# Two gated linear-attention blocks on one core: a rewrite with pk^T x in place of V, queries modulo 5, and a fixed instruction order of its own

## The chip, the cores and the metric

The kernel runs on 1 core of one Trainium2 chip. The time is device microseconds (us) of that core, the median of several executions. The core has five engines that run side by side: PE (TensorE, matmuls), DVE (VectorE), ACT (ScalarE), POOL (GpSimd) and SP (SyncE, which here only starts DMA transfers). A DMA can be started from SP or ACT, which feed hardware queues, or from POOL, which feeds a software queue. The span is the time from the first to the last instruction in the profile of one execution.

## The reference

Two blocks A and B take the same input x (2048 rows, 640 columns, bf16), each with weights of its own. There are 32 heads of 20 columns, and the attention is linear, so no softmax over rows.

```python
g = sigmoid((x * gate_w).sum(-1))                 # one gate per row
for X in (A, B):
    q, k, v = split(x @ wqkv_X)                   # 640 -> 3 x 640, 32 heads of 20
    phi = lambda t: where(t > 0, t + 1, exp(t)) + 1e-6
    pq, pk = phi(q), phi(k)
    kv  = einsum("sd,se->de", pk, v)              # per head, 20 x 20
    z   = pk.sum(rows)                            # per head, 20
    o   = (pq @ kv) / (pq @ z + 1e-6)
    out_X = o @ wo_X
out = g * out_A + (1 - g) * out_B
```

## The kernel before

It projects Q, K and V, keeps V in bf16, and forms K^T V per group of heads. K^T V is masked to its head blocks and multiplied by Wo into one matrix WP per block, so that the output is one product of scaled Q and WP. The scale (gate over denominator) has one value per head and row. A matmul with a 0/1 matrix ("expansion") spreads it over the 20 columns of each head, and DVE multiplies Q by it.

```python
# x transposed by DMA: 4 blocks of 512 rows, 5 instructions of 128 columns each, on SP
for c in range(NCC):
    prs.append((XT[:, c, 512*b : 512*b+512], xin[512*b : 512*b+512, 128*c : 128*c+128]))
# gate_w (1.2 KB) is queued on SP behind the first five of them; PE begins with it
# K and V together: 1280 columns per row tile, in groups of 512, 512 and 256
[(XT[:, c, xcols], WKV[:, c, 0:512]) for c in range(NCC)]      # ... and 512:1024, 1024:1280
# z: ones^T pk on PE;  K^T V: V^T pk on PE, 5 windows x 16 row tiles
[(V16[:, t, 128*c : 128*c+128], PK[:, t, lo:hi]) for t in range(NSC)]
# expansion on PE, scaling on DVE from PSUM
[(CB16[:, EB_OFF+128*k : EB_OFF+128*k+128], RB[X][:, b, :])]
```

Each engine is given its instructions in one fixed order, and the semaphore waits come from a helper that records who reads and writes what. All matmuls therefore carry the helper's line, L296.

## Time and profile before

| before | value |
|---|---|
| time | 254.73 us median of 3 (253.84 to 254.8) |
| span in the profile | 251.6 us |
| PE busy | 225.6 us, 90% of the span |
| DVE busy, ACT busy | 137.5 us, 96.6 us |
| matmuls | 1571 |

These are lines of the page of the kernel before: busy time, the span in 40 slices (each digit is tenths of a slice), and the engines' shares of the chain of waits that ended last.

```profile
span 251.6 us, 3909 instructions
PE 225.6 (90%) x1571; PEld 120.2 (48%) x1571; DVE 137.5 (55%) x323; ACT 96.6 (38%) x207; POOL 7.3 (3%) x11
PE   0499999999999999899999788987976399999995
PEclk9999999999999999999999999999999689999999
PE 82%; DVE 11%; SPq 2%; issue 2%; ACT 1%; DMA 1%; ACTq 0%; DVEq 0%
```

PE is the engine to relieve. Three stretches have holes: the first 10 us, a shallow one from 131 to 185 us (PE busy 47.8 of 54 us), and the digits 9763 near 190 us. The view of busy time by stretches puts numbers on them. Its columns are the stretch, its length, busy us of PE, weight loads, DVE, ACT and POOL (with counts), the granted clock, the DMA share and GB/s.

```profile
0.00:10.00 10.00, 0.53 (x4) 0.32 (x4) 0.46 (x4) 1.28 (x1) 7.32 (x11) 1.00 0.76 200
131.00:185.00 54.00, 47.80 (x374) 27.24 (x371) 34.35 (x82) 20.82 (x50) 0.00 (x0) 1.00 0.00 1
185.00:200.00 15.00, 9.23 (x111) 4.17 (x111) 12.82 (x35) 4.34 (x9) 0.00 (x0) 0.88 0.00 0
200.00:249.00 49.00, 48.17 (x335) 26.39 (x335) 13.98 (x32) 9.55 (x16) 0.00 (x0) 0.97 0.15 51
```

The timeline of the output stage shows what a matmul costs when nothing holds it up (start, us, engine, line, what, count).

```profile
204.90 1.24 PE L296 MATMUL ps<-WPA,PQA 128*128 128x512 bf16 x5
205.97 1.24 PE L296 MATMUL ps<-WPB,PQB 128*128 128x512 bf16 x5
207.05 0.44 PE L296 MATMUL ps<-WPA,PQA 128*128 128x128 bf16 x5
207.33 0.44 PE L296 MATMUL ps<-WPB,PQB 128*128 128x128 bf16 x5
207.61 0.59 PE L296 MATMUL ps<-RBB,CB 128*128 128x512 bf16 x2
```

Read the starts, not the durations, since matmuls overlap. Five of 512 columns start 1.07 us apart, 215 ns each. Five of 128 columns start 0.28 us apart, 56 ns each. A pair of 512 and 128 columns is thus 0.271 us.

### The profile page before, as it was taken

Reading aid. Unit: us, or ns where it says so; the run is one execution under the profiler, and the core shown is the slowest. Engines: PE = TensorE matmul, PEld = TensorE weight load, DVE = VectorE, ACT = ScalarE, POOL = GpSimd, SP = SyncE. Lnnn points to the kernel's source line nnn. Section 1 sums busy time; section 2 is a strip of 40 time slices with the busy share of each in tenths; the row PEclk is TensorE's granted clock in tenths of the full one; section 3 lists DMA queues with packets and bytes.
Section 4 is the critical chain, followed back from the end, with each engine's and each line's share of the span. In section 5 each row is a group of like instructions: output and inputs, shape, how many; then the busy total and the mean of one; then the engine's idle time right before and its main releaser. Section 6 shows DMA issues by size and latency. Waiting matters only on the chain.

```text
span 251.6 us, 3909 instructions
## 1 busy us (share of the span) xinstructions
PE 225.6 (90%) x1571; PEld 120.2 (48%) x1571; DVE 137.5 (55%) x323; ACT 96.6 (38%) x207; POOL 7.3 (3%) x11
## 2 busy tenths in 40 slices
PE   0499999999999999899999788987976399999995
PEld 0244445555555449445555444543853055555553
DVE  0159996345345873596478686774359814242300
ACT  2045555665665530256655445452033011211111
POOL 8300000000000000000000000000000000000000
PEclk9999999999999999999999999999999689999999
DMA  7644694000000700000000000000000001111121
GB/s 217 143 103 101 153 384 168 1 0 0 3 0 0 261 3 0 3 0 0 3 3 0 0 3 0 0 3 0 0 3 0 3 26 52 54 54 52 55 78 52
DMA packets 17219, 12.43 MB, mean 49 GB/s; under 512 B 11249, under 2 KB 15858, under 8 KB 17202
## 3 DMA queue, kind: packets, MB, share of 16 engines
q1 hardware_dynamic: 16466, 10.98, 14.6%
q10 hardware_dynamic: 656, 0.82, 1.1%
q0 software_dynamic: 80, 0.39, 0.4%
q8 instruction: 12, 0.20, 0.3%
q14 instruction: 5, 0.04, 0.1%
HBM read 6.94 MB, written 2.62 MB: 38 GB/s over the span
## 4 chain that ended last, share of the span: by engine, by line
PE 82%; DVE 11%; SPq 2%; issue 2%; ACT 1%; DMA 1%; ACTq 0%; DVEq 0%
PE ps L296 82%; SPq L284 2%; DVE RBB L671 2%; DVE PK L519 2%; DVE RC L640 1%; DVE PQA L726 1%; DVE PQB L726 1%; DVE EK L510 1%; DMA GWROW<-in_gate_w_dram 1%; ACT EK L489 1%; DVE WPB L708 1%; DVE PK L533 0%; DVE RBA L658 0%; DVE ZBD L611 0%; ACT DT L633 0%
## 5 line engine op out<-in xcount | busy, mean ns | idle before, releaser
L296 PE MATMUL ps<-WKV,XT 128*128 128x512 bf16 (+1 forms) x480 | 88.8, 344 | 0.0
L296 PEld LDWEIGHTS ps<-WKV,XT 128*128 128x128 bf16 x480 | 46.7, 98 | 41.2
L417 ACT ACTIVATE EQ<-ps 128x512 bf16<-128x512 f32 x40 | 23.9, 597 | 43.2 <-PE ps L296 39.3
L510 DVE TENSOR_SCALAR EK<-EK 128x640 bf16<-128x640 bf16 x32 | 10.5, 327 | 38.3 <-ACT EK L489 38.3
L482 ACT ACTIVATE EK<-ps 128x512 bf16<-128x512 f32 x32 | 19.1, 597 | 26.0 <-PE ps L296 18.0
L296 PE MATMUL ps<-WPA,PQA 128*128 128x512 bf16 (+1 forms) x160 | 28.0, 307 | 0.8 <-DVE PQB L726 0.8
L296 PE MATMUL ps<-WPB,PQB 128*128 128x512 bf16 (+1 forms) x160 | 27.2, 301 | 0.0
L760 ACT ACTIVATE OSTG<-ps 128x512 bf16<-128x512 f32 x16 | 9.6, 597 | 45.0 <-PE ps L296 45.0
L296 PE MATMUL ps<-XT,WQA 128*128 128x512 bf16 x100 | 24.9, 411 | 0.0
L767 DVE CAST OSTG<-ps 128x128 bf16<-128x128 f32 x16 | 4.7, 292 | 35.0 <-PE ps L296 35.0
L519 DVE SCALAR_TENSOR_TENSOR PK<-ps,EK 128x512 bf16<-128x512 f32 x32 | 22.1, 692 | 1.1
L296 PE MATMUL ps<-XT,WQB 128*128 128x512 bf16 x100 | 21.9, 379 | 0.3 <-DVE ZBD L611 0.3
L296 PEld LDWEIGHTS ps<-WPA,PQA 128*128 128x128 bf16 x160 | 13.5, 99 | 13.0 <-DVE PQB L726 1.3
L296 PEld LDWEIGHTS ps<-WPB,PQB 128*128 128x128 bf16 x160 | 13.1, 99 | 9.9 <-issue 0.8
L296 PEld LDWEIGHTS ps<-XT,WQA 128*128 128x128 bf16 x100 | 10.1, 104 | 13.2 <-issue 3.5
L424 DVE TENSOR_SCALAR EQ<-EQ 128x512 bf16<-128x512 bf16 x40 | 11.5, 288 | 8.7 <-ACT EQ L417 7.0
L496 ACT ACTIVATE V<-ps 128x384 bf16<-128x384 f32 x32 | 15.7, 490 | 1.0
L296 PEld LDWEIGHTS ps<-XT,WQB 128*128 128x128 bf16 x100 | 9.7, 98 | 11.7 <-DVE ZBD L611 0.4
L489 ACT ACTIVATE EK<-ps 128x128 bf16<-128x128 f32 x32 | 8.9, 277 | 15.4 <-PE ps L296 14.9
L433 DVE SCALAR_TENSOR_TENSOR PQB<-ps,EQ 128x512 bf16<-128x512 f32 x20 | 13.8, 692 | 0.7
L433 DVE SCALAR_TENSOR_TENSOR PQA<-ps,EQ 128x512 bf16<-128x512 f32 x20 | 13.8, 692 | 0.7
L726 DVE TENSOR_TENSOR PQA<-PQA,ps 128x512 bf16<-128x512 bf16 x20 | 12.9, 680 | 1.0 <-PE ps L296 1.0
(54 smaller groups left out, 166.5 us busy)
## 6 DMA issues: line engine op xcount, KB each, us to landing
out_dram<-OSTG SPq DMA_DIRECT2D x16, 160.0 KB, 1.8
WKV<-in_A_wqkv_dram SPq DMA_DIRECT2D x1, 1600.0 KB, 7.1
WKV<-in_B_wqkv_dram SPq DMA_DIRECT2D x1, 1600.0 KB, 6.8
WQA<-in_A_wqkv_dram ACTq DMA_DIRECT2D x1, 800.0 KB, 4.9
WQB<-in_B_wqkv_dram SPq DMA_DIRECT2D x1, 800.0 KB, 8.7
WOA<-in_A_wo_dram SPq DMA_DIRECT2D x1, 800.0 KB, 10.4
WOB<-in_B_wo_dram SPq DMA_DIRECT2D x1, 800.0 KB, 12.4
CB<-kconsts POOLq DMA_DIRECT2D x1, 380.0 KB, 6.1
```

The costliest lines, as they stand in the source:

```text
L284: ins = engobj.dma_start(o_ap, i_ap, transpose=transpose)
L296: ins = pe.matmul(out_ap_fn(), l, r, start=(i == 0), stop=(i == n - 1), tile_position=tile_position)
L417: lambda e, bank=bank, slot=slot: e.activation(EQ16[:, slot, :], PS[bank][:, 0:512], ACT.Exp),
L424: lambda e, slot=slot: e.tensor_scalar(EQ16[:, slot, :], EQ16[:, slot, :], 1.0, EPS, op0=ALU.min, op1=ALU.add),
L433: lambda e, bank=bank, slot=slot, k=k, b=b, X=X: e.scalar_tensor_tensor(out=PQ[X][:, k, 512 * b : 512 * b + 512], in0=PS[bank][:, 0:512], ...
L482: lambda e, bA=bA, slot=slot: e.activation(EK16[:, slot, 0:512], PS[bA][:, 0:512], ACT.Exp),
L489: lambda e, bB=bB, slot=slot: e.activation(EK16[:, slot, 512:D], PS[bB][:, 0:128], ACT.Exp),
L496: lambda e, bB=bB, t=t: e.activation(V16[:, t, 0:384], PS[bB][:, 128:512], ACT.Copy),
L510: lambda e, slot=slot: e.tensor_scalar(EK16[:, slot, :], EK16[:, slot, :], 1.0, EPS, op0=ALU.min, op1=ALU.add),
L519: lambda e, bA=bA, slot=slot, t=t: e.scalar_tensor_tensor(out=PK[:, t, 0:512], in0=PS[bA][:, 0:512], scalar=0.0, in1=EK16[:, slot, 0:512], ...
L726: lambda e, bank=bank, X=X, k=k, b=b: e.tensor_tensor(out=PQ[X][:, k, 512 * b : 512 * b + 512], in0=PQ[X][:, k, 512 * b : 512 * b + 512], ...
L760: lambda e, f0=f0, slot=slot: e.activation(OSTG[:, slot, 0:512], PS[f0][:, 0:512], ACT.Copy),
```

## The change

The intent is fewer columns through PE, and an order in which PE doesn't wait. A small scheduler inside the kernel assigns costs to all instructions, simulates the engines, fixes each engine's order, and leaves out waits that are already implied by others. Before any data has landed, PE runs seven matmuls on a tile of ones (L378, "warm-up"). The parts that matter here:

```diff
-# K and V projected together, V copied to SBUF, K^T V = V^T pk
+# only K is projected: 640 columns as 512 + 128 (L423, L424)
+e.matmul(a[:, 0:512], l, WK[X][:, c, 0:512], ...); e.matmul(a[:, 512:D], l, WK[X][:, c, 512:D], ...)
+# G = x^T pk, once per block (L563, L564)
+l = XN[:, t, 128 * c : 128 * c + 128]
+e.matmul(a[:, 0:512], l, PKt[X][:, t, 0:512], ...); e.matmul(a[:, 512:D], l, PKt[X][:, t, 512:D], ...)
+# K^T V of six exact head groups of 120 columns = Wv^T G, masked on the way out of PSUM (L581)
+e.matmul(PS[0:GR, ps.slot, GR*i : GR*i+GR], WV[X][:, c, lo:lo+GR], GS[X][:, c, lo:lo+GR], ...)
... [cut: WP = KVL x Wo, written to DRAM and read back with rows modulo 5]
-# z by ones^T pk on PE, gate by matmuls on PE
+# z by 30 additions on DVE, gate by 16 multiply-and-sum on DVE
-# expansion by matmul, 40 products from PSUM
+# Q columns modulo 5 (weights read with step 5), so that a scale of 32 heads is repeated 4 times
+WQ[X][:, c, g::5]                                              # L650
+# both denominators of two row blocks in four column tiles of PE at once (L721)
+# scale goes to DRAM and comes back repeated; 8 products of 128x2560 in SBUF (L777)
+# loads at the start
+dma("SP", "x0", ...); dma("SP", "x1", ...)          # 256 rows, transposed on PE
+for c in range(NC): dma("ACT", "wkA%d" % c, ...)    # K weight of A, 5 x 160 KB, hardware queue
+dma("POOL", "wkB", ...)                             # K weight of B, 800 KB, software queue
+xt_dma(256, 512); xt_dma(512, 1024); xt_dma(1024, 1536); xt_dma(1536, 2048)
+                                                    # each one transposing DMA of all 640 columns
... [cut]
+for X in XS:
+    for g in range(NC): q_unit(X, 3, g)
+out_unit(0); den(1)
+for t in range(1, NT): out_unit(t, t == NT - 1)
```

## The prediction

> **What bounds the kernel now.** TensorE. The page's first part has PE busy 225.6 of 251.6 us (90%), DVE 55%, ACT 38%; the chain of waits is 82% PE, 11% DVE. The stretches view gives three losses: PE busy 0.5 us of the first 10 us (nothing starts until gate_w has landed behind five transposes), 47.8 of 54 us in 131-185 (the chain there: exp, PK, expansion products, reciprocals on DVE), 9.2 of 15 us in 185-200 (reciprocals 0.95 us, 32-row products 0.29 us, expansion). Granted clock 0.986.
>
> In steady state the timeline shows five 512-column matmuls starting every 1.07 us (215 ns each) and five 128-column ones every 0.28 us (56 ns), each with new weights, so weight loads hide. The Trainium skill ("TensorE: Matmul & The Clock Gate", "Wait - 56ns, not 53.3ns?") states 215.7 and 55.6 ns; the trace agrees. PE work is therefore columns, about 0.42 ns each.
>
> **What the change does.** Columns before: K and V 204,800, Q 102,400, output 102,400, K^TV 23,000, z row sums 20,500, denominators 20,500, expansion 20,500, WP 16,600, gate 10,200: about 521,000. V is no longer projected and copied out (ACT loses 27.8 us); pk^T x (G) costs 102,400 instead, Wv^T G 7,200. z sums go to DVE (30 adds), the gate to DVE (16 reductions), expansion to DMA through DRAM, denominators are four column tiles at once, WP has exact 120-row head groups. After: K, G, output 480 pairs of 512+128 at 0.271 = 130 us; Q 200 x 0.215 = 43; WP 3.3; Wv^T G 60 small ones 3.3 to 6 (120-column weights; the skill's "Weight-path perf modes" gives fast weight load only at 128; no run here shows it); denominators 2 to 6; z 0.5. Sum about 184; with 1.5% for imperfect streaming (the K/V stage ran 88.8 us against 86 by count) 187 us.
>
> DVE stays near 137 us, an estimate: z adds 30 x 0.8 and gate 16 x 0.9 us are new; expansion products 26 us become 8 of about 1.5; the 32-row products vanish; K and Q post-processing stay. In K it is 1.16 of 1.36 us per tile, in G it absorbs gate and z, in Q 0.98 of 1.08. The first reciprocal of 512 columns (4 x 0.95 = 3.8 us) and the first scalings land inside Q, so DVE falls about 8 us behind; eight PSUM banks and one output tile hide part; the second denominator, waiting for the last Q tile, shows the rest.
>
> **Critical path.** PE still carries it. Start: x, constants and both K weights (2 MB at the 200 GB/s of the first 10 us) make PE lose about 7 us instead of 10. Stalls at Q to output about 4 us. Tail 2.7 us as now. Span 7+187+4+3 = 201 us; timed runs stood 3 us above the span before, but the block wrapper goes: 202 us.
>
> **Right or wrong.** PE busy 185-190 us; no wait above 1 us between 12 us and the end of Q; the 185-200 hole gone; K, G and output each about 0.27 us per pair; PE idle behind DVE PQ before the second denominator, 0 to 8 us; DVE share near 68%; clock near 1.
>
> **What would make it wrong.** Pairs slower than 0.271 us when 512 and 128 alternate (0.03 us each is 14 us); weights read with step 5 loading too slowly to hide; a fixed instruction order that misfits real durations; DRAM round trips longer than the 19 us of work over them.
>
> Predicted 202 us, 80% range 194 to 212; faster 0.98, same 0.015, slower 0.005.

## The result, and the profile after

The changed kernel takes 212.76 us median of 4 (212.39 to 215.04); in the same comparison the kernel before took 254.28 us (253.72 to 254.8). The ratio is 0.8395 (95% interval 0.8351 to 0.8439). Ratios here are the mean time of one kernel's fast runs over that of the other's of the same rounds, so they are not quite the ratio of the medians. A run counts as slow when it lies more than 1.5% above the fastest of the same kernel, and only fast runs are compared; all these are fast. The sign and most of the gain were foretold, but the time lies 0.8 us above the stated range and 10.8 us above the point.

The page after:

```profile
span 211.6 us, 3143 instructions
PE 190.0 (90%) x1311; PEld 105.9 (50%) x1311; DVE 134.1 (63%) x231; ACT 75.2 (36%) x116; POOL 1.8 (1%) x7
PE   5402999999999999999999999999966899999995
PEclk9955699999999999999999999999999999999999
PE 76%; DVE 12%; DMA 9%; ACTq 1%; issue 0%; ACT 0%; DVEq 0%
```

PE's busy time fell by 35.6 us, about as counted. The hole near 190 us became a smaller one (the digits 668, now at 153 to 169 us). But the start has a new hole: 5402, with a clock of 5 tenths behind it, and a DMA that takes 9% of the chain. The waits of PE, by who ended them (total us, times, longest):

```profile
PE ps L423 <- DMA WKW<-in_A_wqkv_dram: 12.6, 3, 10.9
PE ps L650 <- DVE PKB L676: 2.1, 1, 2.1
PE ps L820 <- DVE PKB L676: 1.9, 1, 1.9
PE ps L721 <- DVE PKB L676: 0.7, 1, 0.7
```

The largest is for the K weight of A, 10.9 us at a stretch. The timeline shows PE around it:

```profile
8.92 0.22 PE L424 MATMUL ps<-WKW,XT 128*128 128x128 bf16 x1
20.03 0.61 PE L423 MATMUL ps<-WKW,XT 128*128 128x512 bf16 x1 [10.89 <-DMA WKW<-in_A_wqkv_dram]
20.54 0.63 PE L423 MATMUL ps<-WKW,XT 128*128 128x512 bf16 x1
24.81 0.38 PE L423 MATMUL ps<-WKW,XT 128*128 128x512 bf16 x1
25.08 0.38 PE L423 MATMUL ps<-WKW,XT 128*128 128x512 bf16 x1
```

When the work resumes, a pair of 512 and 128 columns takes about 0.52 us instead of 0.27, and this lasts until 24.7 us. The Trainium skill ("TensorE: Matmul & The Clock Gate", "What's actually happening") states that PE runs at 1.2 instead of 2.4 GHz after an idle window of about 3.4 us, until it has been busy for about as long. The trace agrees in kind: half the clock is granted from 11.0 us, and full clock again at 24.7 us, 4.7 us after the work resumed (0.4 us of them idle). It does not show an idle time of 3.4 us as a threshold: the clock fell only 1.9 us after the last matmul had ended, when PE had worked for 0.7 of the last 3.4 us. So a wait on a DMA can cost more than its length, here about 2 us more.

The stretches view of the same start, with the columns as before (clock, DMA share and GB/s last):

```profile
2.00:6.00 4.00, 3.25 (x18) 1.26 (x17) 0.47 (x2) 1.59 (x2) 0.78 (x1) 1.00 0.99 246
6.00:10.00 4.00, 1.91 (x12) 0.80 (x12) 0.10 (x1) 0.56 (x2) 0.00 (x0) 1.00 1.06 81
10.00:14.00 4.00, 0.00 (x0) 0.00 (x0) 0.00 (x0) 0.00 (x0) 0.00 (x0) 0.63 1.06 100
14.00:18.00 4.00, 0.00 (x0) 0.00 (x0) 0.00 (x0) 0.00 (x0) 0.00 (x0) 0.50 1.31 80
18.00:22.00 4.00, 1.53 (x5) 0.52 (x6) 0.00 (x0) 0.00 (x0) 0.00 (x0) 0.50 1.19 172
22.00:26.00 4.00, 4.00 (x21) 2.06 (x20) 2.21 (x4) 2.00 (x3) 0.00 (x0) 0.66 1.13 215
```

The DMA share is 1 or more while only 80 to 100 GB/s move: the engines are occupied but move little. I call this the crawl. In the packet records between 6 and 20 us the median transposing packet takes 18 ns but the mean is 146 ns, and times of packets on one engine overlap, which is why the share can exceed 1; I take the long times for waiting. The loads' entries tell which suffer (size, median us from issue to landing):

```profile
WKW<-in_A_wqkv_dram ACTq DMA_DIRECT2D x5, 160.0 KB, 6.6
WKW<-in_B_wqkv_dram POOLq DMA_DIRECT2D x1, 800.0 KB, 19.7
XT<-in_A_x_dram SPq DMA_TRANSPOSE x4, 12.9
```

**The account.** The K stage ends at 64.6 us. Its own work is 160 pairs, 43.4 us at 0.271, so 21.2 us were lost before and inside it. The prediction had 7. All that follows took 147.0 us, where the prediction had 150.6 (143.6 of PE work, 4 of stalls, 3 of tail). The span was missed by 10.6 us: the start cost 14.2 us more than predicted, and 3.6 us less after it hid part of that, by luck. The excess is in the start alone.

### The profile page after: what moved, and what is told of

It is laid out like the page before. It is cut to its first block, busy times and chain, and to the rows that moved or that the text cites. A ratio compares the mean times of both kernels' runs of the same rounds, so it can differ in the third digit from the quotient of the medians.

```text
span 211.6 us, 3143 instructions
## 1 busy us (share of the span) xinstructions
PE 190.0 (90%) x1311; PEld 105.9 (50%) x1311; DVE 134.1 (63%) x231; ACT 75.2 (36%) x116; POOL 1.8 (1%) x7
## 4 chain that ended last, share of the span: by engine, by line
PE 76%; DVE 12%; DMA 9%; ACTq 1%; issue 0%; ACT 0%; DVEq 0%
PE ps L820 19%; PE ps L563 16%; PE ps L423 16%; PE ps L650 11%; DMA WKW<-in_A_wqkv_dram 9%; PE ps L564 4%; PE ps L424 4%; DVE PKB L676 3%; DVE PKA L676 3%; DVE EQ L668 2%; DVE RCT L751 2%; PE ps L581 2%; DVE PKB L777 1%; DVE PKA L777 1%; PE ps L616 1%; PE ps L721 1%
## 5 line engine op out<-in xcount | busy, mean ns | idle before, releaser
L423 PE MATMUL ps<-WKW,XT 128*128 128x512 bf16 x160 | 45.8, 391 | 12.6 <-DMA WKW<-in_A_wqkv_dram 12.6
L424 PE MATMUL ps<-WKW,XT 128*128 128x128 bf16 x160 | 35.7, 223 | 0.0
L436 ACT ACTIVATE EK<-ps 128x640 bf16<-128x640 f32 x32 | 22.4, 703 | 36.4 <-PE ps L424 36.4
L423 PEld LDWEIGHTS ps<-WKW,XT 128*128 128x128 bf16 x160 | 16.0, 100 | 33.4 <-DMA WKW<-in_A_wqkv_dram 12.2
L820 PE MATMUL ps<-WPA,PKA 128*128 128x512 bf16 (+1 forms) x160 | 24.5, 299 | 1.9 <-DVE PKB L676 1.9
L820 PE MATMUL ps<-WPB,PKB 128*128 128x512 bf16 (+1 forms) x160 | 24.5, 299 | 0.0
L439 DVE TENSOR_SCALAR EK<-EK 128x640 bf16<-128x640 bf16 x32 | 10.4, 325 | 20.2 <-ACT EK L436 20.2
L842 ACT ACTIVATE OST<-ps 128x640 bf16<-128x640 f32 (+1 forms) x16 | 11.1, 696 | 32.2 <-PE ps L820 32.2
L563 PE MATMUL ps<-PKB,XN 128*128 128x512 bf16 x80 | 22.3, 379 | 0.0
L563 PE MATMUL ps<-PKA,XN 128*128 128x512 bf16 x80 | 21.8, 379 | 0.0
L820 PEld LDWEIGHTS ps<-WPA,PKA 128*128 128x128 bf16 x160 | 12.3, 98 | 12.1 <-issue 2.8
L564 PE MATMUL ps<-PKA,XN 128*128 128x128 bf16 x80 | 17.5, 219 | 0.0
L564 PE MATMUL ps<-PKB,XN 128*128 128x128 bf16 x80 | 17.5, 219 | 0.0
L424 PEld LDWEIGHTS ps<-WKW,XT 128*128 128x128 bf16 x160 | 16.0, 100 | 0.0
## 6 DMA issues: line engine op xcount, KB each, us to landing
WKW<-in_B_wqkv_dram POOLq DMA_DIRECT2D x1, 800.0 KB, 19.7
```

Source lines behind the costliest of these rows:

```text
L423: e.matmul(a[:, 0:512], l, WK[X][:, c, 0:512], start=(c == 0), stop=(c == NC - 1))
L424: return e.matmul(a[:, 512:D], l, WK[X][:, c, 512:D], start=(c == 0), stop=(c == NC - 1))
L436: op("ACT", lambda e: e.activation(EK[:, ek.slot, :], psw(ps, D), ACT.Exp), act_cost(D), ins=[ps], outs=[ek], name="ke")
L439: lambda e: e.tensor_scalar(EK[:, ek.slot, :], EK[:, ek.slot, :], 1.0, EPS, op0=ALU.min, op1=ALU.add),
L563: e.matmul(a[:, 0:512], l, PKt[X][:, t, 0:512], start=(t == 0), stop=(t == NT - 1))
L564: return e.matmul(a[:, 512:D], l, PKt[X][:, t, 512:D], start=(t == 0), stop=(t == NT - 1))
```

## The experiments

The question is why the K weights landed so late. In the first 2.6 us three streams are issued: transposes on SP, five pieces of K of A on ACT's hardware queue, and K of B on POOL's software queue. Theory C: plain loads and transposing loads slow each other. Theory F: the form is at fault, one transposing DMA of all 640 columns instead of five of 128. Theory S: the software queue is at fault when it runs beside transposes. Theory Q: the K weights are slow by themselves.

A helpful check runs through all of them. For a variant of the changed kernel, span minus the end of the K stage is the rest, and whatever changes only the start leaves the rest at 147.0 us.

### e1: transposes after the K weights

```diff
+WKL = [w for k in bwk for w in bwk[k].writers]        # the K weight loads
 dma("SP", "xt%d" % r0, ..., transpose=True, after=WKL)
+# ... after=WKL also on what SP issues next, so that SP's order stays
```

> The four transposing loads (and what the sync queue issues after them) wait until both K weights have landed; nothing else changes. Theory C (plain loads and transposing loads slow each other whenever they are in flight together): both K weights land by about 8 to 9 us instead of 21.7, the K stage streams from about 6 us with one gap of 1 to 3 us for the first transposed columns, and the span falls from 211.6 to 197-203 us. Rival Q (the K weights are slow by themselves: five 160 KB pieces on one queue and 800 KB on the software queue): they still land at 17 us or later and the span is 211 us or more, plus the delay of the transposes.

Measured: span 199.0 us, time 201.27 us (two runs), ratio to before 0.7931. The K weights landed by 9.9 us, the K stage ended at 52.0 us, and the rest was again 147.0 us. Theory C gets its number, and theory Q is out: without transposes beside it the software load took 7.6 us instead of 19.7. The start's stretches:

```profile
2.00:6.00 4.00, 3.55 (x17) 1.57 (x16) 0.29 (x1) 1.47 (x2) 0.79 (x1) 1.00 0.93 296
6.00:10.00 4.00, 2.76 (x20) 1.32 (x19) 0.29 (x1) 0.79 (x2) 0.00 (x0) 1.00 0.53 206
14.00:18.00 4.00, 4.00 (x31) 2.28 (x30) 3.12 (x7) 1.44 (x3) 0.00 (x0) 1.00 1.09 207
```

The plain loads now run at 296 GB/s, the transposes later at about 207 GB/s, and the clock stays full.

### e2: transposes in five pieces

```diff
-XT[:, :, r0:r1]  <-  x[r0:r1, :]
+for c in range(5): XT[:, c, r0:r1]  <-  x[r0:r1, 128*c : 128*c+128]
```

> Each transposing load is cut into five of 128 columns, the form of the kernel before; order and queues stay. Theory F (the form with five column blocks in one instruction is what holds the DMA engines; in the kernel before 256-byte packets of the cut form took 18 ns beside a weight load): packets of the transposes take about 18 ns from the start, K weights land by 9 us, span 196-202 us. Theory C (any overlap of transposes with plain loads is slow): K weights still land at 15 us or later and the span stays within 3 us of 211.6.

Measured: span 205.4 us, time 207.36 us; the last K weight let PE go on at 13.3 us, the K stage ended at 58.4 us, the rest 147.0 us. Neither theory got its number: the crawl is shorter, not gone. The five-piece form also issues slowly (29.4 us of SP for the same rows, against 11.3 in e1), which leaves gaps for others. That this is why it was milder is an argument, not shown.

### e3: K of B on the hardware queue

```diff
-dma("POOL", "wkB", WK["B"], ...)
+dma("ACT", "wkB", WK["B"], ...)
```

> The K weight of B is issued from the scalar engine's hardware queue behind the five pieces of A, instead of from the software queue; all else stays. Theory S (the software queue's packets[...] hold up the rest): pieces 3 and 4 of A land before 10 us, span 197-203 us. Theories C and F: pieces 3 and 4 still land at 15 us or later, span 209-214 us.

Measured: span 200.2 us, time 201.54 us. The K stage ended at 53.2 us, the rest 147.0 us. One load differs from the changed kernel: it is on another queue, and there it stands behind the five pieces of A. Transposes are in flight from 4.5 us as before, and the crawl is gone:

```profile
6.00:10.00 4.00, 2.39 (x18) 1.27 (x17) 0.29 (x1) 0.79 (x2) 0.00 (x0) 1.00 1.20 217
10.00:14.00 4.00, 2.59 (x21) 1.31 (x19) 2.21 (x4) 1.43 (x3) 0.00 (x0) 1.00 1.16 240
```

Where the changed kernel moved 81 and 100 GB/s, this moves 217 and 240. This speaks for theory S and against C and F, which had foretold 209 to 214 us. It also says that starting the transposes this early was not wrong in itself.

### e4: the kernel before with one-piece transposes

```diff
-for c in range(NCC): prs.append((XT[:, c, 512*b:512*b+512], xin[512*b:512*b+512, 128*c:128*c+128]))
+prs.append((XT[:, :, 512*b:512*b+512], xin[512*b:512*b+512, :]))
```

> The kernel before with each block of 512 rows transposed by one instruction of five column blocks, as after the change, instead of five instructions; a wait counts one completion instead of five. Theory F: its Q weight of A, in flight beside the first transposes, lands later than the 4.9 us of before, the transposes' packets take far over 18 ns while it is in flight, and the first block lands later, so that the start grows by some us. Theory C or S: the start stays as it was within 1 us (254 us).

Measured: span 253.4 us, time 254.95 us, ratio 1.0046 (same). The Q weight landed after 5.0 us against 4.9, and the last transpose ended at 17.9 us instead of 29.0. Theory F is out as a cause by itself; the one-piece form is even the faster one.

### e5 and e6: a software-queue load in the kernel before

```diff
-wq_op["A"] = dma_op("ACT", "wqa", ...)
+wq_op["A"] = dma_op("POOL", "wqa", ...)     # e5: with one-piece transposes; e6: with five pieces
```

> The kernel before with one-piece transposes (the run with those alone kept its start) and with its first weight load, 800 KB for Q of A, moved from the scalar engine's hardware queue to the software queue. Theory S (a load on the software queue and one-piece transposes in flight together slow each other, in any kernel): the transposes' packets take over 60 ns in the mean while the load lasts, the load lands at 12 us or later instead of 5.7, and the first Q matmuls start that much later than 10.2 us; span 256-266 us. Rival P (it was a matter of how many loads the changed kernel starts at once, 2 MB in 2 us): the load lands by 9 us, and the span stays at 252-255 us.

> The kernel before with only its Q weight of A moved to the software queue; transposes in five pieces as they were. Theory S with the one-piece form as a condition: milder than in the run with both, the load lands by 8 to 11 us, transposes' packets under 50 ns, span 251-257 us. If the software queue alone is to blame, it is as bad as with one-piece transposes.

Measured: e5 span 251.5 us, time 254.48 us; e6 span 253.9 us, time 255.96 us. Neither crawled, so theory S as I had put it ("in any kernel") failed here. The trace's packets show that the two kinds hardly met: in e5 they did from 4 to 6 us, when the first transposing DMA was nearly through; the software load moved alone from 6 to 8 us, and the next transposes came at 8. In e6 only 131 KB of transposes moved between 4 and 8 us, beside 1,075 KB of software loads. The run did not test what it was meant to test. It does show that a short meeting costs nothing.

### e9, e10, e11, e12: which queues must meet

e9 takes all K weights to the software queue (two queues in flight instead of three). e11 holds K of B back until K of A has landed. e10 adds to e4 an 800 KB load on the software queue, ahead of all else there, which that kernel needs only later. e12 is e10 with that one load on ACT's hardware queue instead.

```diff
 # e9
-dma("ACT", "wkA%d" % c, ...)
+dma("POOL", "wkA%d" % c, ...)
 # e11
-dma("POOL", "wkB", ...)
+dma("POOL", "wkB", ..., after=[w for c in range(NC) for w in bwk["A", c].writers])
 # e10 (e12: "ACT"), on e4; moved to the front of the queue
-wq_op["B"] = dma_op("SP", "wqb", ...)
+wq_op["B"] = dma_op("POOL", "wqb", ...)
```

> The changed kernel with the five pieces of K of A moved to the software queue too, ahead of K of B: two queues in flight (transposes on one, all weights on the other) instead of three; bytes and order of issue stay. Theory T (three queues in flight at once, one of them transposing and one the software queue, is what crawls; in the runs with two of them nothing crawled): K of A lands by 9 us, K of B by 13 us, transposes' packets stay under 50 ns in the mean between 4 and 14 us, span 198-204 us. Theory S (software queue beside one-piece transposes): K weights land at 16 us or later, as in the changed kernel, span 207-216 us.

> The kernel before with one-piece transposes and, on the software queue ahead of its constants, an 800 KB load that it needs only later (Q of B), so that transposes, a weight load of the scalar engine's queue and an 800 KB load of the software queue are in flight together from the first microsecond. Theory T: the crawl appears in the other kernel as well; the load that takes 5.0 us there with one-piece transposes alone lands at 9 us or later, transposes' packets take over 60 ns in the mean between 4 and 14 us, the first Q matmuls start after 13 us. If the load lands by 7.5 us and the transposes' packets stay under 35 ns, theory T is false as stated.

> The changed kernel with the software queue's load of K of B held back until K of A has landed, so that never more than two queues carry large loads. Theory T: K of A lands by 9 us, then K of B lands within 8 us of its issue, transposes' packets under 50 ns in the mean; span 200-206 us. Theory S: K of A lands early, but K of B takes over 12 us beside the transposes; span over 208 us.

> The control of the run with three queues in the kernel before (span 264.5, gate_w landing 14.9 us after its issue): the same extra 800 KB, but on the scalar engine's hardware queue behind the first 800 KB. Theory S (the software queue beside transposes makes the crawl): gate_w lands by 11 us after the start, transposes' packets under 45 ns in the mean between 4 and 14 us, span 251-256 us. Theory C (any plain bytes beside one-piece transposes crawl alike): gate_w lands after 16 us and the span is 258 us or more.

Measured: e9's one fast run took 212.53 us (its other run and its profile were slow, so I use no more of it than that it did not recover). e11: span 212.0 us, time 212.5 us, no better than the change. Both missed what theory T, that three queues are needed, had foretold. In e11 K of B, alone with the transposes, took 10.4 us from its issue at 12.1 us. But e11's time proves little, since most of its loss comes from holding the load back: with the 7.6 us of e1, K of B would have landed at 19.7 instead of 22.5 us (an estimate from the two traces). K of A, on the hardware queue beside transposes, was late in e11 too: PE could go on with its last piece only at 11.1 us (9.6 in e3). e11's waits:

```profile
PE ps L424 <- DMA WKW<-in_B_wqkv_dram: 10.0, 1, 10.0
PE ps L424 <- DMA WKW<-in_A_wqkv_dram: 3.1, 1, 3.1
```

e10: span 264.5 us, time 264.64 us, ratio 1.0437. e12: span 253.7 us, time 255.97 us, ratio 1.0092. The same 800 KB, needed just as late, cost 10.8 us of span on the software queue against ACT's queue, where they stand behind the first 800 KB and cost hardly anything (e4, without moving this load: 253.4). e10 is also the plainest case against theory T: the last packet of ACT's load began at 5.1 us, so from 6 us on only two queues were in flight, and it crawled. e10's start, then e12's, stretches as before:

```profile
6.00:10.00 4.00, 0.00 (x0) 0.00 (x0) 0.00 (x0) 0.00 (x0) 3.20 (x2) 1.00 1.20 133
10.00:14.00 4.00, 0.00 (x0) 0.00 (x0) 0.00 (x0) 0.00 (x0) 0.00 (x0) 1.00 1.22 166
14.00:18.00 4.00, 0.00 (x0) 0.00 (x0) 0.00 (x0) 0.00 (x0) 0.00 (x0) 1.00 1.60 76
```

```profile
6.00:10.00 4.00, 0.00 (x0) 0.00 (x0) 0.00 (x0) 0.00 (x0) 2.20 (x2) 1.00 1.11 326
10.00:14.00 4.00, 1.89 (x8) 0.85 (x9) 0.77 (x5) 0.00 (x0) 0.00 (x0) 1.00 1.14 241
```

In e10, what PE waited for was not the added load but gate_w, 1.2 KB, which sat in SP's queue behind the first transposes, and its wait in e12 was back to 2 us above that of e4 (9.7 us). e10's wait, then e12's:

```profile
PE ps L296 <- DMA GWROW<-in_gate_w_dram: 20.7, 1, 20.7
```

```profile
PE ps L296 <- DMA GWROW<-in_gate_w_dram: 11.7, 1, 11.7
```

From the packet records of the traces, over the stretch in which the kinds met (a transposing packet is 256 bytes; e13 is described below):

| run | stretch, us | beside the transposes | mean ns of a transposing packet | all, GB/s |
|---|---|---|---|---|
| e13 | 10 to 18 | nothing | 20 | 206 |
| e3 | 4 to 12 | hardware queue | 36 | 232 |
| e12 | 4 to 10 | hardware queue, 389 KB software | 20 | 329 |
| e11 | 6 to 12 | hardware queue | 37 | 143 |
| e11 | 16 to 22 | software queue | 59 | 168 |
| e10 | 6 to 20 | software queue | 97 | 118 |
| changed kernel | 6 to 20 | hardware and software queue | 146 | 99 |

The median is 18 ns in every row: most packets take no longer than alone, and a minority of long ones makes the mean (in the changed kernel 365 of 1,248 took over 200 ns).

What is shown: in the kernel before, moving one 800 KB load between the two queues decides between crawl and no crawl (e10 against e12), and in the changed kernel likewise (e3). It also suffices not to let them meet (e1). Two things move with the queue and were not separated from it: the load's place (on ACT's queue it stands behind other weights) and its packets, 5,120 bytes on the software queue against 1,280 on ACT's. Against place as the whole cause speaks e11, where the software load came after K of A and the mean packet still took 59 ns, though milder than the 146 ns of the changed kernel. The compute engines can hardly have held the software queue up: in the changed kernel DVE and POOL were idle from 10 to 22 us, in e10 from 10 to 18. What stays open: the inner reason; why e11 moved no more than 143 GB/s beside a hardware-queue load where e3 moved 232; and how long or how full the meeting must be, since e5, e6 and e12 had a short one for nothing.

### e7 and e8: from Q to output

The second term of the prediction was a wait at the end of Q because DVE is behind. Both runs stand on e1.

```diff
 # e7
-out_unit(0); den(1)
+out_unit(0); out_unit(1); out_unit(2); den(1)
 # e8, in addition: scaling of the second row block of Q behind other DVE work
+prio=LOW if j >= 2 else None, name="pqs"
```

> On top of the run whose transposes wait for the K weights (span 199.0): the second denominator is computed after the third output tile instead of after the first. My account of the Q to output stage (VectorE is behind; the denominator waits for its last Q tile): of the 4.7 us in which PE waits there, the 2.1 us inside Q stay, the 2.6 us before the denominator go; span 196-197. Rival (the output tiles themselves wait, for scaled Q or for WP): the wait moves to an output tile, and the span stays at 199 within 0.7 us.

> On top of the late denominator: the scaling of the second block of Q (2 x 1.4 us of VectorE) goes behind the Q tiles' own work instead of ahead of it. If VectorE's order is what empties PSUM too late, PE's 2.1 us wait inside Q falls below 0.7 us and the span is 194-196. If VectorE's sum of work there is the bound and not its order, nothing changes against the late denominator alone.

Measured: e7 span 197.6 us, time 199.52 us, ratio 0.7857; e8 span 195.1 us, time 196.71 us, ratio 0.7755. The waits of PE on DVE from Q on, those above 0.5 us, e7 first, then e8:

```profile
PE ps L653 <- DVE PKB L679: 2.1, 1, 2.1
PE ps L823 <- DVE PKB L679: 1.9, 1, 1.9
```

```profile
PE ps L824 <- DVE PKB L679: 1.4, 1, 1.4
```

e7 missed its number. The denominator's wait had been only 0.7 us; the other 1.9 us is the first output tile's own, and it stayed (the rest fell from 147.0 to 146.6 us; the remainder of the gain is an earlier end of K, 51.1 us). That tile waits on a DVE instruction that reads Q out of PSUM. I take it for a wait on a free pair of PSUM banks, which no run tested. e8 hit: four products of 1.4 us in a row had kept DVE from emptying PSUM. With two of them moved back, the 2.1 us wait is gone and the rest is 143.4 us. It was the order of DVE's work, not its sum.

### e13: both cures

```diff
 # on e8
-dma("POOL", "wkB", WK["B"], ...)
+dma("ACT", "wkB", WK["B"], ...)
```

> The best so far (transposes after the K weights, late second denominator, late scaling: 196.7 us, span 195.1) with K of B moved to the hardware queue behind K of A. If K of B's landing is now a matter of bytes (2 MB before the first transpose), nothing moves by more than 1 us: span 194.3-195.8. If the software queue still costs by its later start, K of A lands earlier and up to 1.5 us are won.

Measured: span 194.6 us, time 195.77 us median of 4 (195.59 to 196.56), ratio to before 0.7725 (0.7689 to 0.7761). Against e8 the difference is within what a start may scatter. This is the fastest correct version tried, 17 us below the changed kernel's median:

```profile
span 194.6 us, 3146 instructions
PE 188.9 (97%) x1311; PEld 106.3 (55%) x1311; DVE 134.2 (69%) x231; ACT 75.2 (39%) x116; POOL 1.0 (0%) x6
PE   6999999999999999999999999999997999999995
```

PE is now busy 97% of the span, so what is left to gain by order is little.

## Why the prediction was right or wrong

**PE work is columns: right.** 187 us were predicted, 190.0 us of busy time measured, of which 3.0 us are seven warm-up matmuls and about 2 us the half clock (some 8 pairs at 0.52 instead of 0.27 us). That leaves 185 us, so the count of 184 was good and the 1.5% added to it was hardly needed. Pairs of 512 and 128 columns do run at 0.27 us. From 64.6 us on, everything took 147.0 us against 150.6 predicted. By columns, pk^T x costs what the V projection cost (102,400); the gain comes from what goes with it and around it: K^T V, z, expansion, denominators, WP, gate.

**Small and odd weights: right, at the low end.** The 60 matmuls of Wv^T G took two times 1.65 us, and four column tiles did 20 matmuls of 512 columns in 1.22 us. Loads of 120-column weights took 135 ns and those with step 5 117 ns, against 98 ns, and both hid behind matmuls.

**DVE load: right.** 134.1 us against 137. Its share is 63% and not 68% only because the span was longer; e13 shows 69%.

**Stalls from Q to output: right in size, half right in cause.** 4.7 us against 4. The second denominator waited only 0.7 us; 1.9 us was the first output tile and 2.1 us PSUM that DVE did not empty in time (e7, e8).

**The start: the step that failed.** It reads: "x, constants and both K weights (2 MB at the 200 GB/s of the first 10 us) make PE lose about 7 us instead of 10." It cost 21.2 us. I divided bytes by a rate, and took the rate from a start in which no large software-queue load met long transposes. In the changed kernel 99 GB/s moved between 6 and 20 us. PE waited 12.6 us for K of A and then ran at half clock until 24.7 us. With the transposes in flight as early and the load on another queue (e3) the loss is 9.8 us (53.2 minus 43.4), with the transposes held back (e1) 8.6, in e13 7.8. So the sum was 1 to 3 us too low for a start without the crawl, and 14.2 us too low with it. The prediction also said that no wait above 1 us would come between 12 us and the end of Q; there was one of 10.9 and one of 2.1. The list of what could make the prediction wrong did not name the loads at the start.

**The wrapper.** The timed run that was profiled stood 1.3 us above its span (212.94 and 211.6); 1 us was assumed. The prediction's 3 us for the kernel before set a median against the span of another run: for one run, it is 1.8 us (253.44 and 251.6).

## What to carry to other kernels

Estimate a start by which loads meet, not by bytes over a rate: keep large loads off the software queue while transposing DMAs are in flight, or hold the transposes back until the first weights have landed, and look for a DMA share near 1 with a low GB/s. When an engine has a little slack, the order of its work decides: what frees buffers for the busiest engine goes first, and what is needed only later goes behind. A stretch in which nothing was changed (here the 147.0 us after K) is a good control: if it stays, the cause lies elsewhere.

## What the Trainium skill lacked or had wrong

- "DMA: Bandwidth & Descriptors", "Issuing engines are not separate DMA queues", says that DMAs started from the scalar, sync or gpsimd engine run on the same 16 DMA engines and interleave, regardless of who started them. Here the starter mattered: the same 800 KB beside one-piece transposes gave a span of 264.5 us from POOL and 253.7 us from ACT (e10, e12). No page that I read warns that a software-queue load and transposing DMAs slow each other to about 100 GB/s.
- The same page, "Latency and other measured facts", gives 261 GB/s for transposing DMAs with a non-contiguous middle dimension. Alone or nearly so, they moved 206 GB/s in e13 (10 to 18 us) and 250 GB/s in e12 (10 to 16 us), so the figure was nearly reached but not held. It does not say that one instruction for all five column blocks ends sooner than five (17.9 against 29.0 us for 2048 rows, e4 against before).
- "TensorE: Matmul & The Clock Gate", "LDWEIGHTS (loading the stationary operand)", gives columns divided by 1.2 in ns. The traces show 98 ns for 128 columns, 96 ns for 32 (the denominators' weights) and 135 ns for 120, so the time does not follow the number of columns; all were hidden behind matmuls. For 120 against 128 columns this fits what the prediction quotes on fast weight load, which that section leaves out.
- The same page, "Measured speedup vs the span model", lists three column tiles of 512 columns (2.38 times), but not four. Four took 1.22 us for 20 matmuls here, against 4.3 us at 215 ns each, which is 3.5 times.
